# Attention with a memory beside a SiLU layer: products issued in halves, seven score-weight buffers, and a new order of the pieces

## The chip, the cores and the metric

The kernel runs on one core of a Trainium2 chip. The metric is the device time of one execution in microseconds (us). The page of the profile and its trace come from one execution of the kernel before, with every instruction's time. The engines are named as the profile names them: PE (TensorE, matrix products), PEld (its weight loads), DVE (VectorE), ACT (ScalarE), POOL (GpSimd) and SP (SyncE, which here issues nearly all DMAs).

## The reference, cut to what matters

The input x has 2048 rows of 512 numbers. After a layer norm, two branches read it; their sum and x are the output.

```
xn = layernorm(x)
# branch A: 32 heads of 16, four segments s of 512 rows
q, k, v = xn @ wq, xn @ wk, xn @ wv
for s in range(4):                       # M and z begin at 0
    a_dot = softmax(q_s k_s^T / 4 + causal mask) @ v_s
    a_mem = (phi(q_s) @ M) / (phi(q_s) @ z + 1e-6)
    o_s   = g * a_mem + (1 - g) * a_dot      # g = sigmoid(beta)
    M, z  = M + phi(k_s)^T @ v_s, z + sum(phi(k_s))
# branch B
h = silu(xn @ w1)                        # 512 -> 1792
out = x + o @ wo + h @ w2
```

phi(t) is t + 1 for t > 0 and exp(t) otherwise. All inputs are bf16.

## The kernel before, in words

**Tiles.** The 2048 rows are 16 tiles of 128; four tiles make a segment. xnT holds the normed input transposed, four blocks of 128 features on the partitions. The first four tiles are transposed by PE, the other twelve by DMA. "Head group" dt (0 to 3) is a block of 128 features of q, k or v, thus eight heads.

**Pieces.** All work is cut into pieces, each a small function. The string ORDER (lines 16 to 98) lists them by name, and a loop at the end (line 715) calls them one by one. Each engine executes its own instructions in exactly the order in which the pieces were called; semaphores between engines are added by the framework, which also gives out buffers. So ORDER, written out by hand, decides what stands behind what on every engine and in SP's queue. The names:

- `v`, `k`, `q`, `h` (s.i): a projection or first-layer unit of segment s: a 128x512 result in one PSUM bank, summed over four full products (128x128 weights, 512 columns; lines 301 and 332).
- `kv`/`ka`, `qv`/`qa`, `vv`/`va`: DVE or ACT copies that result out of the bank (lines 316, 326, 338). For k, POOL also makes a copy with the even heads' rows zeroed (kTo, line 317).
- `ha`: ACT takes tanh of a unit (line 419). `hv`: DVE makes silu of it into hT (line 424) and thereby frees the bank.
- `S` t: scores. Four 32-row groups of PE work side by side on 512 columns into psS, a single PSUM tile of four banks (line 597), and ACT takes the exponential of all of it into a weight buffer Pb (line 604, 128x2048, 80 of them). POOL sets the masked part to 0 (line 612). t = 20 s + 5 dt + b; the five batches b of a head group are the even and odd heads against the four key tiles.
- `E`, `O` n: weighing of even or odd heads of head group n = 4 s + dt: 16 small products of Pb and v into one bank (line 631). `Ev`/`Ea`, `Ov`/`Oa` copy it out and move the softmax sums by DMA (lines 646, 654, 661, 665).
- `fp`, `fa`, `fv` and `gp`, `ga`, `gv`: phi of k and of q on POOL, ACT and DVE. `t`: a DMA transposes phi(k). `m`: 8 products for M (line 381). `mv`, `mw`: DVE adds and masks M. `s`, `sv`: sums phi(q) z.
- `r`, `w` and, in the last segment, `R`, `W`: reciprocals and gate on DVE. `z`, `d`: DMAs that spread these factors over the partitions (line 504, two issues each). `zv`, `dv`: DVE multiplies with them. `n`, `nv`: one product with M and its addition on DVE (lines 530, 537).
- `o` s.j.i: one full product of the output of tile j in segment s: i = 0 to 13 is the unit hT[i] with w2, i = 14 to 17 the head group i - 14 with wo (line 572). 18 of them make an output tile. `xl`: loads x again. `st`: DVE adds x (line 550) and SP stores it (line 553).
- `xs`, `xg`, `Nv`, `X`, `XD`: layer norm statistics, root, normed tile, transposes by PE or DMA.

**Buffers.** Four PSUM banks (pool pp, tag "pb", function bank) serve all results of `v k q h E O m s n o` in turn; the other four are psS. In the last segment the output tiles j = 2 and 3 are gathered in two banks of psS, as the scores no longer need it (lines 560 to 565). Five buffers Pb (line 619) are given out by the order: `S` takes the first of a list, and the last weighing that reads a buffer puts it back.

**Around the change** the order is this: some 20 full products come ahead of the first score piece; then score pieces follow with other pieces between them, one small ACT job to nearly each; behind the last score piece (S79) come the rest of the units, the last two weighings and 78 output products, with the last segment's memory part.

Of the kernel before, what the change touches and what calls it, by code (L numbers as in the profile page):

```python
# [10 lines left out]
BF16 = mybir.dt.bfloat16  # L11
# [5 lines left out]
busy41 xs0 xg0.1 xs1 xg1.1 Nv0 X0.1 Xa0.1 busy10 xs2 xg2.1 xs3 xg3.1 v0.0 Nv1 X1.1 Xa1.1 Nv2 X2.1 Xa2.1 Nv3 X3.1 Xv3.1 v0.1 va0.0 odd k0.0 xs7 q0.0 qv0.0 q0.1 ka0.0 xs4 fa0.0  # L17
S1 xs5 q0.2 vv0.1 k0.2 kv0.2 qa0.1 fp0.2
S0 ones0 xs6 v0.3 fa0.2 xs8 xg4.4 vv0.3 qv0.2 h0.4
S3 xs11 k0.1 h0.7 ha0.7 kv0.1 xs9 hv0.7  # L20
S2 h0.10 Nv5 ha0.4 Nv4 XD4 v0.2 vv0.2
S4 h0.5 zeros fp0.1 ha0.10 Nv6 XD6 E0 xs10 hv0.4 XD5
S7 h0.2 Ev0 hv0.10 q0.3 ha0.5 xg8.4 fv0.2 fp0.0
S6 hv0.5 Nv7 XD7 O0 v1.1 Ov0 ha0.2 qv0.3
S5 xs14 h0.0 ha0.0 hv0.2 kind vv1.1 h0.1 fv0.0 Nv10
S9 k1.2 XD10 q1.3 kv1.2 ha0.1
S12 hv0.0 t0.0 k0.3 Nv11 E1 fa0.1 xs15 qv1.3 hv0.1 Ev1 kv0.3
S8 h0.11 Nv8 ha0.11 t0.2 ones1 tanh k1.1
# [12 lines left out]
S20 m0.0 sv0 xg12.4 ha1.4 o0.0.9 o0.0.12 r0.1 hv1.8 r0.3 k2.1 t0.3 mv0.0 r0.2
S24 kv2.1 o0.0.7 hv1.4 h1.0 E4 r0.0 ha1.0
S26 Ev4 o0.0.3 h1.1 O4 hv1.0 ha1.1 Nv15
S29 w0 z0.1 o0.0.13 gv1.1 z0.3 Ov4 k2.0 z0.2 h1.10 ha1.10 Nv12 kv2.0
S25 XD12 hv1.1 gp1.0 m0.2 h1.5 hv1.10 zv0.3 fp1.0 ha1.5 h1.13
S27 o0.0.8 mv0.2 v2.1 hv1.5 Nv13 z0.0 ha1.13 vv2.1 v2.0
S28 hv1.13 h1.6 E5 gv1.0 vv2.0 Ev5 ha1.6 hv1.6 o0.0.17 fp1.3
S32 v2.2 vv2.2 h1.2 o0.1.1 ha1.2 zv0.2
S34 o0.1.4 h1.3 XD15 hv1.2 o0.1.10 fa1.3 zv0.0 O5
S30 o0.1.2 zv0.1 xl0.0 o0.0.14 Ov5 fv1.3 o0.1.5 o0.1.11 o0.2.17 o0.0.15 fp1.2 o0.2.1 o0.1.3 o0.0.16 ha1.3  # L50
S31 o0.2.16 o0.1.14 fa1.2 o0.2.2 t1.1 XD13 Nv14 o0.2.15 hv1.3 o0.1.15 v2.3 st0.0
S33 vv2.3 q2.3 fa1.0 o0.2.11 o0.1.6 E6 fv1.2 qv2.3
S38 Ev6 h1.12 ha1.12 o0.1.16 o0.2.7 fp2.1 O6 Ov6
S36 o0.2.3 hv1.12 mw0.2 fa2.1 o0.2.9 o0.2.5 fv1.0 o0.2.12 xl0.3 q2.2 o0.1.13 xl0.2 qv2.2
S37 t1.3 o0.2.14 q2.0 ga1.2 o0.2.4 o0.3.7 qv2.0 o0.1.17 o0.2.8
S35 k2.3 o0.2.0 o0.3.0 o0.2.6 o0.2.10 fv2.1 gp1.3 ga1.3 t1.2 mw0.0 o0.3.13
S39 o0.1.7 gp1.2 o0.2.13 t1.0 o0.3.9 o0.1.12 o0.1.0 o0.3.8 kv2.3 gv1.3 E7
S41 Ev7 o0.3.17 o0.3.5 o0.1.9 XD14 o0.3.10 o0.1.8 st0.1 o0.3.15 o0.3.1 o0.3.4 ga2.3 o0.3.2
S40 O7 xl1.3 gv1.2 gp2.3 m1.2 o0.3.11 o0.3.14 fa2.2 st0.2 mv1.2 s1
S42 m1.0 Ov7 gv2.3 mv1.0 o0.3.16 o0.3.3 q3.1 qv3.1 o0.3.6 sv1 t2.1  # L60
S43 q3.3 fa2.0 qv3.3 o0.3.12 o1.1.12 fp2.0 st0.3 E8 r1.2
S44 v3.1 r1.0 q3.0 r1.3 va3.1 Ev8 o1.1.9
S46 r1.1 fv2.0 o1.1.3 w1 fp2.2 o1.1.6 z1.3 h2.8 qv3.0 O8 d1.3 ha2.8 hv2.8 t2.0
S47 h1.7 ha1.7 d1.2 o1.1.10 k3.0
S45 o1.1.8 Ov8 kv3.0 hv1.7 v3.2 k3.1 zv1.3 d1.1 ga2.2 vv3.2
S48 h2.3 z1.1 gp2.0 kv3.1 fv2.2 dv1.3 ha2.3 fp2.3 v3.0 o1.1.13
S49 vv3.0 n1.3 fa2.3 o1.1.5 hv2.3 nv1.3 v3.3 E9
S50 o1.1.17 h2.0 ha2.0 vv3.3 h2.2
S52 o1.1.0 o1.1.7 fv2.3 Ev9 xl1.2 k3.2 dv1.1 ha2.2 hv2.0 d1.0 zv1.1 mw1.2 kv3.2 hv2.2 z1.0 O9 z1.2
S54 Ov9 t2.2 o1.1.4 o1.0.0 o1.1.11 o1.1.2 q3.2 o1.0.13  # L70
S51 o1.0.7 qv3.2 n1.1 h2.4 o1.0.11 dv1.0 zv1.0 dv1.2 ha2.4 o1.0.17 gp2.2 o1.0.10
S53 o1.0.3 xl1.0 xl1.1 o1.0.9 nv1.1 o1.0.1 o1.0.6 hv2.4 n1.0 o1.0.2 nv1.0 E10 Ev10 zv1.2 ga2.0
S55 h2.11 o1.1.1 n1.2 ha2.11 nv1.2 o1.0.4 hv2.11 o1.1.15 gv2.2 mw1.0 o1.0.8
S56 O10 o1.1.16 h2.7 o1.0.5 Ov10 ha2.7
S58 hv2.7 o1.0.16 o1.1.14 gv2.0 o1.3.1 o1.3.10 o1.3.8 o1.3.11 o1.0.14 o1.3.17 o1.3.2 t2.3 ga2.1 gp2.1 st1.1 o1.3.13
S57 h2.1 m2.0 o1.3.7 o1.3.3 mv2.0 o1.0.15 ha2.1
S59 o1.0.12 h2.5 o1.3.6 hv2.1 st1.0 ha2.5 E11
S60 h2.6 o1.3.14 gv2.1 ha2.6 gp3.3 Ev11 hv2.5 O11 s2
S61 o1.3.0 xl2.2 Ov11 o1.3.12 hv2.6 o1.2.17 xl3.0 o1.2.8 sv2 r2.0 o1.3.9 h2.10 r2.2 gp3.1 ha2.10
S64 o1.2.16 o1.2.12 o1.3.5 o1.2.6 h2.12 ha2.12 hv2.10 o1.2.14 r2.3 o1.3.4  # L80
S62 h2.9 ha2.9 o1.2.9 o1.3.15 o1.2.4 o1.2.13 r2.1 o1.3.16 o1.2.2 o1.2.10 hv2.12 w2 d2.1
S63 d2.2 o1.2.3 hv2.9 o1.2.5 m2.2 st1.3 ga3.3 o1.2.1 z2.1 fill o2.2.12 d2.0 E12 mv2.2
S67 o2.2.1 o1.2.11 Ev12 h2.13 O12 gv3.3 dv2.1 ha2.13 Ov12 hv2.13
S66 o1.2.0 o2.2.7 o1.2.15 n2.1 dv2.0 o1.2.7 o2.2.3 o2.2.11 o2.2.13 o2.2.6 z2.2 o2.2.9
S65 st1.2 o2.2.4 o2.0.1 h3.4 o2.0.11 ha3.4 zv2.1 dv2.2 nv2.1 d2.3 z2.0 o2.0.6 o2.0.9 hv3.4 z2.3
S69 gp3.0 h3.3 ha3.3 o2.2.2 o2.2.5 E13 Ev13
S68 o2.2.10 o2.0.4 hv3.3 o2.2.0 h3.0 ha3.0 n2.2 o2.2.8 xl3.1 o2.0.8 zv2.2 nv2.2
S73 o2.0.10 k3.3 o2.2.16 hv3.0 ka3.3 h3.1 ha3.1 dv2.3 zv2.0
S70 hv3.1 O13 o2.0.0 zv2.3 o2.0.7 o2.0.3 n2.3 o2.0.13 o2.0.12 Ov13 o2.2.15 nv2.3 ga3.1
S71 n2.0 h3.2 nv2.0 o2.0.5 o2.1.11 o2.1.2 mw2.2 o2.2.17 xl2.0 gv3.1 o2.2.14 ha3.2 ga3.2 o2.0.16  # L90
S72 o2.1.8 o2.0.14 o2.0.15 st2.2 h3.5 mw2.0 ha3.5 gp3.2 o2.1.0 o2.0.2 o2.1.10
S74 hv3.2 ga3.0 o2.1.12 hv3.5 o2.1.5 o2.0.17 o2.3.3 o2.1.7 o2.3.7 gv3.2 st2.0 E14
S76 o2.3.5 gv3.0 o2.1.16 o2.1.3 xl2.3 o2.3.12 o2.3.0 Ev14 O14 s3 xl2.1 Oa14
S75 o2.3.2 o2.1.1 sv3 h3.9 o2.3.10 h3.10 r3.0 ha3.9 ha3.10
S77 o2.1.15 r3.2 r3.1 r3.3 o2.1.14 o2.3.1 w3 hv3.9 hv3.10 o2.3.4 h3.11 ha3.11 o2.3.13 o2.3.8
S78 o2.3.9 o2.3.11 d3.3 R0.1 o2.1.9 d3.1 hv3.11 R0.2 h3.12 R0.0 R0.3 o2.3.15 o2.3.16 ha3.12 o2.1.17
S79 E15 W0 d3.0 hv3.12 o2.1.6 o2.1.4 z3.2 o2.3.6 h3.7 Ea15 o2.1.13 o2.3.14 st2.1 h3.13 ha3.7 hv3.7 dv3.3 ha3.13 o3.3.0 o3.3.1 hv3.13 O15 dv3.0 o2.3.17 h3.8 ha3.8 z3.0 d3.2 dv3.1 o3.2.4 o3.0.3 o3.0.2 Ov15 o3.0.11 h3.6 o3.3.3 hv3.8 ha3.6 o3.3.4 zv3.2 st2.3 o3.1.0 xl3.2 o3.1.10 hv3.6 o3.1.9 o3.1.13 o3.2.7 R1.2 n3.1 o3.1.11 o3.0.4 o3.1.6 R1.1 o3.2.8 o3.1.3 dv3.2 o3.3.13 o3.0.7 o3.2.13 o3.3.11 o3.2.10 n3.2 z3.1 o3.0.0 o3.0.8 R1.0 o3.3.8 o3.2.11 zv3.0 o3.0.5 nv3.2 o3.1.8 R1.3 W1 o3.1.4 o3.3.12 n3.0 o3.0.9 o3.0.6 o3.3.9 nv3.0 o3.3.5 o3.2.9 o3.1.5 o3.1.14 z3.3 o3.2.16 o3.0.10 o3.2.12 o3.0.16 o3.3.2 zv3.1 nv3.1 n3.3 zv3.3 o3.2.0 nv3.3 xl3.3 o3.0.15 o3.3.6 o3.0.13 o3.1.16 o3.0.1 o3.1.15 o3.0.17 o3.2.6 o3.0.12 o3.0.14 o3.3.7 st3.0 o3.3.16 o3.3.17 o3.3.14 o3.1.12 o3.3.10 o3.3.15 o3.2.14 o3.2.3 o3.2.5 o3.1.17 o3.1.7 o3.1.2 o3.2.15 o3.1.1 st3.3 st3.1 o3.2.1 o3.2.2 o3.2.17 st3.2
# [4 lines left out]
def kernel(  # L102
# [196 lines left out]
    def mm4(ps, w_sb, cols, rhs):  # L299
        for ki in range(DT):  # L300
            nc.tensor.matmul(  # L301
                ps[:, :], lhsT=w_sb[:, ki, cols], rhs=rhs(ki), start=(ki == 0), stop=(ki == DT - 1)
            )

    def dense(s, w_sb, i):

        ps = bank([P, L], F32, "ps")
        mm4(ps, w_sb, slice(i * P, (i + 1) * P), lambda ki: xnT[:, ki, s * L : (s + 1) * L])
        return ps

    def k_mm(s, dt):
        sts[s]["k", dt] = dense(s, wk_sb, dt)
# [9 lines left out]
    def q_mm(s, dt):  # L322
        sts[s]["q", dt] = dense(s, wq_sb, dt)
# [4 lines left out]
    def v_mm(s, j):  # L328
        t = s * TPS + j
        ps = sts[s]["v", j] = bank([P, L], F32, "ps")  # L330
        for ki in range(DT):
            nc.tensor.matmul(  # L332
                ps[:, :], lhsT=xnT[:, ki, t * P : (t + 1) * P], rhs=wv_sb[:, ki, :],
                start=(ki == 0), stop=(ki == DT - 1),
            )
# [76 lines left out]
    def h_mm(s, ft):  # L412
        if "hT" not in sts[s]:
            sts[s]["hT"] = hpool.tile([P, FT, L], BF16, name="hT", tag="hT")
        sts[s]["h", ft] = dense(s, w1_sb, ft)
# [333 lines left out]
```

## Time and profile before

| | us |
|---|---|
| median of three runs (lowest, highest) | 235.81 (235.72, 236.08) |
| the profiled execution | 235.23 |
| its span, from the first instruction to the last | 233.4 |
| PE busy, of the span | 219.8 |
| ACT busy; of it the 80 exponentials at 1.877 | 196.4; 150.1 |
| DVE busy | 171.5 |
| POOL busy | 117.4 |
| first exponential begins, last begins | 13.40, 206.73 |
| last product begins | 229.71 |

Busy time of PE joins overlapping products: one 128x512 product shows 0.38 us from its start to its end, but in a run of them the next starts 0.2157 us later. In the timeline a row has the start, the length, the engine, the line of the kernel, and in brackets the idle time ahead of it with what ended that. In a table of stretches the columns are PE, PEld, DVE, ACT and POOL busy (with the number of instructions), granted clock of PE, share and rate of the DMAs. A row of waits has the sum, the number and the longest.

### The profile page before, as it was taken

Reading aid. Unit: us, or ns where it says so; the run is one execution under the profiler, and the core shown is the slowest. Engines: PE = TensorE matmul, PEld = TensorE weight load, DVE = VectorE, ACT = ScalarE, POOL = GpSimd, SP = SyncE. Lnnn points to the kernel's source line nnn. Section 1 sums busy time; section 2 is a strip of 40 time slices with the busy share of each in tenths; the row PEclk is TensorE's granted clock in tenths of the full one; section 3 lists DMA queues with packets and bytes.
Section 4 is the critical chain, followed back from the end, with each engine's and each line's share of the span. In section 5 each row is a group of like instructions: output and inputs, shape, how many; then the busy total and the mean of one; then the engine's idle time right before and its main releaser. Section 6 shows DMA issues by size and latency. Waiting matters only on the chain.

```text
span 233.4 us, 4991 instructions
## 1 busy us (share of the span) xinstructions
PE 219.8 (94%) x1845; PEld 94.2 (40%) x1879; DVE 171.5 (73%) x343; ACT 196.4 (84%) x172; POOL 117.4 (50%) x181
## 2 busy tenths in 40 slices
PE   7998798999999999999999999999999999999993
PEld 7533333433343443333434333344443334344440
DVE  3588999765689887767697887855775695868843
ACT  2478899999999999999999998999998999983000
POOL 4348767674448763546757766345624535440000
PEclk9999999999999999999999999999999999999998
DMA  6999532113101122204432121321130312132211
GB/s 203 369 376 344 128 32 51 26 36 68 37 9 31 49 67 60 58 31 97 113 59 68 47 80 55 75 53 53 52 98 26 101 36 87 41 93 69 90 56 69
DMA packets 34632, 20.38 MB, mean 87 GB/s; under 512 B 15664, under 2 KB 34096, under 8 KB 34608
## 3 DMA queue, kind: packets, MB, share of 16 engines
q1 hardware_dynamic: 34320, 19.80, 30.2%
q8 instruction: 14, 0.23, 0.4%
q10 hardware_dynamic: 288, 0.26, 0.4%
q14 instruction: 10, 0.08, 0.1%
HBM read 9.96 MB, written 2.10 MB: 52 GB/s over the span
## 4 chain that ended last, share of the span: by engine, by line
PE 70%; ACT 12%; DMA 6%; issue 4%; DVE 4%; SPq 2%
PE ps L301 23%; PE psO L572 22%; ACT Pb L604 9%; PE psS L597 9%; PE psV L631 6%; DMA x_hi<-in_A_x_dram 6%; PE ps L332 4%; PE psS L572 3%; ACT th L419 3%; PE psM L381 1%; PE ps L530 1%; DVE stats L269 1%; SPq L176 1%; ACT ex L355 1%; DVE xn_t L283 1%
## 5 line engine op out<-in xcount | busy, mean ns | idle before, releaser
L604 ACT ACTIVATE Pb<-psS 128x2048 bf16<-128x2048 f32 x80 | 150.1, 1877 | 6.4 <-PE psS L597 5.6
L612 POOL TENSOR_SCALAR_AFFINE_SELECT Pb<-Pb 128x512 bf16<-128x512 bf16 (+1 forms) x112 | 81.0, 736 | 81.9 <-ACT Pb L604 80.6
L301 PE MATMUL ps<-xnT,w_sb 128*128 128x512 bf16 x217 | 56.3, 380 | 1.9 <-DVE hT L424 0.7
L572 PE MATMUL psO<-w_sb,hT 128*128 128x512 bf16 x182 | 56.2, 381 | 0.9 <-issue 0.6
L424 DVE SCALAR_TENSOR_TENSOR hT<-th,ps 128x512 bf16<-128x512 bf16 x56 | 37.8, 678 | 13.8 <-ACT th L419 13.4
L419 ACT ACTIVATE th<-ps 128x512 bf16<-128x512 f32 x56 | 33.2, 594 | 4.5 <-PE ps L301 4.4
L572 PEld LDWEIGHTS <-hT 128*128 128x128 bf16 x224 | 20.3, 97 | 27.1 <-issue 7.9
L301 PEld LDWEIGHTS <-w_sb 128*128 128x128 bf16 x224 | 20.4, 98 | 26.1 <-issue 5.5
L631 PE MATMUL psV<-Pb,Vz 128*32 128x384 bf16 (+3 forms) x512 | 23.3, 302 | 0.6 <-DVE Vz L338 0.6
L597 PE MATMUL psS<-qT,kT 16*128 16x384 bf16 (+3 forms) x256 | 17.3, 302 | 2.0 <-ACT Pb L604 0.9
L597 PE MATMUL psS<-qT,kTo 32*128 32x512 bf16 (+3 forms) x256 | 17.2, 300 | 1.7 <-ACT Pb L604 1.0
L572 PE MATMUL psO<-wo_sb,oT 128*128 128x512 bf16 x51 | 17.6, 381 | 0.3 <-issue 0.3
L631 PEld LDWEIGHTS <-Vz 128*32 128x32 bf16 x512 | 10.8, 96 | 17.4 <-issue 7.3
L301 PE MATMUL ps<-xnT,wk_sb 128*128 128x512 bf16 x62 | 16.2, 380 | 0.3 <-DVE oT L537 0.2
L332 PE MATMUL ps<-wv_sb,xnT 128*128 128x512 bf16 x61 | 16.2, 381 | 0.3
L301 PE MATMUL ps<-xnT,wq_sb 128*128 128x512 bf16 x62 | 16.1, 381 | 0.1
L317 POOL TENSOR_SCALAR kTo<-kT,pm_odd 128x512 bf16<-128x512 bf16 x16 | 12.1, 757 | 5.1 <-ACT kT L316 3.4
L661 DVE CAST odd<-psV 128x512 bf16<-128x512 f32 x15 | 10.3, 685 | 4.6 <-PE psV L631 4.6
L654 DVE CAST oraw<-psV 128x512 bf16<-128x512 f32 x15 | 10.3, 684 | 4.0 <-PE psV L631 3.8
L326 DVE CAST qT<-ps 128x512 bf16<-128x512 f32 x15 | 10.2, 683 | 4.0 <-PE ps L301 4.0
L597 PEld LDWEIGHTS <-kT 16*128 16x128 bf16 x256 | 6.1, 91 | 17.0 <-issue 15.7
L550 DVE SCALAR_TENSOR_TENSOR o_out<-psO,x_res 128x512 bf16<-128x512 f32 x14 | 9.6, 685 | 4.3 <-PE psO L572 4.1
(83 smaller groups left out, 225.5 us busy)
## 6 DMA issues: line engine op xcount, KB each, us to landing
w_sb<-in_B_w_dram SPq DMA_DIRECT2D x2, 1792.0 KB
spr<-rz SPq DMA_DIRECT2D x56, 64.0 KB
x_res<-in_A_x_dram SPq DMA_DIRECT2D x16, 128.0 KB
out_dram<-o_out SPq DMA_DIRECT2D x16, 128.0 KB
x_hi<-in_A_x_dram SPq DMA_DIRECT2D x2, 512.0 KB
oraw<-odd SPq DMA_DIRECT2D x64, 16.0 KB
wv_sb<-in_A_wv_dram SPq DMA_DIRECT2D x2, 256.0 KB
wk_sb<-in_A_wk_dram SPq DMA_DIRECT2D x1, 512.0 KB
```

Source lines behind the costliest of these rows:

```text
L301: nc.tensor.matmul(ps[:, :], lhsT=w_sb[:, ki, cols], rhs=rhs(ki), start=(ki == 0), stop=(ki == DT - 1))
L317: nc.gpsimd.tensor_scalar(out=kTo[:, dt, :], in0=kT[:, dt, :], scalar1=pm_odd[:, 0:1], scalar2=1.0, op0=ALU.mult, op1=ALU.mult,)
L332: nc.tensor.matmul(ps[:, :], lhsT=xnT[:, ki, t * P : (t + 1) * P], rhs=wv_sb[:, ki, :], start=(ki == 0), stop=(ki == DT - 1),)
L419: nc.scalar.activation(out=th[:], in_=sts[s]["h", ft][:, :], func=AF.Tanh, scale=0.5)
L424: nc.vector.scalar_tensor_tensor(out=st["hT"][:, ft, :], in0=st.pop(("th", ft))[:], scalar=1.0, in1=st.pop(("h", ft))[:, :], op0=ALU.add, ...
L572: nc.tensor.matmul(st["psO", j], lhsT=lhsT, rhs=rhs, start=len(done) == 1, stop=len(done) == FT + DT)
L597: nc.tensor.matmul(psS[:, g, c0 : c0 + nq], lhsT=kk[rows, dt, kt * P : (kt + 1) * P], rhs=st["qT"][rows, dt, kt * P : L], start=True, stop ...
L604: exp = nc.scalar.activation(out=Pb[:, :, :], in_=psS[:, :, :], func=AF.Exp, scale=SCALE)
L612: mask = nc.gpsimd.affine_select(out=blocks, in_=blocks, compare_op=ALU.is_ge, fill=0.0, base=0, pattern=[[0, blocks.shape[1]], [1, P]], c ...
L631: nc.tensor.matmul(psV[32 * g : 32 * g + 32, kt * P : L], lhsT=Vzs[s % 2][:, kt, 4 * dt + g, par : par + 2, :].rearrange("p a d -> p (a d) ...
L654: copy(out=oraw[:], in_=sts[s].pop(("psV", 0))[:, :])
L661: copy(out=odd[:], in_=sts[s].pop(("psV", 1))[:, :])
```

## The change

1. The pieces `v k q h` are cut in two: `k0.1.0` issues the first two products of a unit, `k0.1.1` the other two; the bank is taken by the first half.
2. There are seven weight buffers Pb instead of five.
3. The products of output tile 2 of the last segment no longer wait for DVE's reading of tile 3, and the other way round: the framework sees the two banks as one tile, and a declaration takes the dependence away.
4. ORDER is written anew. It has the same pieces (those of point 1 in halves), with few exceptions: which engine copies some results (`qa0.0` and `ka0.2` in place of `qv0.0` and `kv0.2`, `qv0.1` in place of `qa0.1`, `ka3.1` and `ka3.2` in place of `kv3.1` and `kv3.2`, `kv3.3` in place of `ka3.3`, `Ov14` and `Oa15` in place of `Oa14` and `Ov15`), and where each piece stands. Behind the last score piece (now S78) stand 87 full products instead of 98.

The functions:

```diff
-    def mm4(ps, w_sb, cols, rhs):
-        for ki in range(DT):
+    def half_mm(s, key, part, lhsT, rhs):
+
+        if part == 0:
+            sts[s][key] = bank([P, L], F32, "ps")
+        for ki in (2 * part, 2 * part + 1):
             nc.tensor.matmul(
-                ps[:, :], lhsT=w_sb[:, ki, cols], rhs=rhs(ki), start=(ki == 0), stop=(ki == DT - 1)
+                sts[s][key][:, :], lhsT=lhsT(ki), rhs=rhs(ki), start=(ki == 0), stop=(ki == DT - 1)
             )
...
-    def k_mm(s, dt):
-        sts[s]["k", dt] = dense(s, wk_sb, dt)
+    def k_mm(s, dt, part):
+        dense(s, "k", wk_sb, dt, part)
...
-        nc.vector.scalar_tensor_tensor(
+        st["out", j] = nc.vector.scalar_tensor_tensor(
...
-        nc.tensor.matmul(st["psO", j], lhsT=lhsT, rhs=rhs, start=len(done) == 1, stop=len(done) == FT + DT)
+        mm = nc.tensor.matmul(st["psO", j], lhsT=lhsT, rhs=rhs, start=len(done) == 1, stop=len(done) == FT + DT)
+        if s == LAST and j >= 2 and ("out", 5 - j) in st:
+            tc.declare_no_dep(mm.ins, st["out", 5 - j].ins, reason="the two outputs lie in banks of their own")
...
-    Pbs = [ppool.tile([P, 4, L], BF16, name=f"Pb{i}") for i in range(5)]
+    Pbs = [ppool.tile([P, 4, L], BF16, name=f"Pb{i}") for i in range(7)]
```

The order, its beginning and its end (the first line's opening, up to `va0.0`, keeps its order but for the halves):

```diff
-... v0.1 va0.0 odd k0.0 xs7 q0.0 qv0.0 q0.1 ka0.0 xs4 fa0.0
-S1 xs5 q0.2 vv0.1 k0.2 kv0.2 qa0.1 fp0.2
-S0 ones0 xs6 v0.3 fa0.2 xs8 xg4.4 vv0.3 qv0.2 h0.4
-S3 xs11 k0.1 h0.7 ha0.7 kv0.1 xs9 hv0.7
-S2 h0.10 Nv5 ha0.4 Nv4 XD4 v0.2 vv0.2
-S4 h0.5 zeros fp0.1 ha0.10 Nv6 XD6 E0 xs10 hv0.4 XD5
+... v0.1.0 v0.1.1 va0.0 odd k0.0.0 k0.0.1 ka0.0 q0.0.0 q0.0.1 xs7 k0.1.0 vv0.1 kind ones0 qa0.0 fa0.0
+S3 k0.1.1 v0.3.0 k0.2.0 k0.2.1 xs5 xs6 ka0.2 xs4 xg4.4 fp0.0
+S4 q0.1.0 kv0.1 v0.3.1 h0.4.0 h0.4.1 ha0.4 vv0.3 hv0.4 zeros Nv5 Nv4
+S0 Nv7 h0.10.0 h0.10.1 Nv6 q0.1.1 v0.2.0 ha0.10 fp0.1
+S2 qv0.1 fv0.0 hv0.10 h0.5.0 XD5 h0.5.1 XD6 v0.2.1 q0.2.0 ha0.5
+S5 vv0.2 q0.2.1 h0.7.0 h0.7.1 xs11 ha0.7 v1.1.0 hv0.5 xs9
+S1 h0.1.0 v1.1.1 qv0.2 xs10 fp0.2 hv0.7 k0.3.0 XD7 h0.1.1 XD4 t0.0 ha0.1
...
+S78 z3.0 dv3.2 h3.6.0 o2.1.1 o2.1.0 zv3.2 h3.6.1 ha3.6 h3.10.0 h3.10.1 d3.1 st2.1 o3.2.7 hv3.6 o3.3.8 o3.3.2 E15 Ea15 zv3.0 O15 o3.1.2 o3.1.11 ha3.10 ... o3.3.17 o3.3.1 st3.3 ... o3.1.17 st3.0 st3.2 st3.1
```

## The prediction

> **What bounds the kernel now.** I read the page first, then the stretches, then the timeline. The page says that TensorE is busy 94% of the span and that its clock is granted in full until the last slice; ACT has 84%.
>
> ```profile
> PE 219.8 (94%) x1845; PEld 94.2 (40%) x1879; DVE 171.5 (73%) x343; ACT 196.4 (84%) x172; POOL 117.4 (50%) x181
> ...
> PEclk9999999999999999999999999999999999999998
> ```
>
> The table of stretches of 5 us shows that this share is a mean over stages: DVE is full at 25 us (4.96 of 5), ACT at 45 us (4.99, while PE has 4.50), and near 145 us PE and ACT together.
>
> ```profile
> 25.00:30.00 5.00, 4.17 (x57) 1.86 (x58) 4.96 (x11) 4.28 (x5) 4.35 (x9) 1.00 0.43 88
> 45.00:50.00 5.00, 4.50 (x46) 1.85 (x45) 2.76 (x6) 4.99 (x5) 3.16 (x5) 1.00 0.09 21
> 145.00:150.00 5.00, 4.95 (x58) 2.10 (x58) 3.71 (x7) 4.99 (x5) 1.67 (x3) 1.00 0.38 91
> ```
>
> The timeline tells why ACT is full. There is one score buffer (psS). PE may write the next scores when the exponential has read the last ones, and meanwhile ACT does one small job (0.59 us):
>
> ```profile
> 45.99 1.88 ACT L604 ACTIVATE Pb<-psS 128x2048 bf16<-128x2048 f32 x1
> ...
> 47.76 0.59 ACT L419 ACTIVATE th<-ps 128x512 bf16<-128x512 f32 x1
> ...
> 47.91 0.40 PE L597 MATMUL psS<-qT,kTo 32*128 32x384 bf16 x8 [0.36 <-ACT Pb L604]
> ...
> 48.36 1.88 ACT L604 ACTIVATE Pb<-psS 128x2048 bf16<-128x2048 f32 x1
> ```
>
> So exponentials start every 2.37 to 2.38 us (45.99, 48.36, 50.73), whatever PE has to do, as long as its work fits between two score pieces. PE here waited 0.36. **The 80 exponentials cut the run into 79 intervals, each as long as the longer of 2.377 and PE's own work in it.**
>
> PE's prices come from intervals above that floor. Intervals with 9, 10 and 11 full products (128x512) take 2.38, 2.59 and 2.81, so a product costs 0.2157 and a score piece 0.44. The interval 40.79 to 43.61 holds a score piece, 8 products and one weighing (E or O): 2.82, so a weighing costs 0.656. Two neighbours (2.53 and 2.46), one of them with 8 products and a memory product (m), give 0.45 for that one; a sums piece (s) is about 0.2. Summed over the words of ORDER:
>
> | intervals | products, before / after | weighings | PE work | paced sum, before / after | measured before |
> |---|---|---|---|---|---|
> | 1-12 | 84 / 94 | 4 / 3 | 26.0 / 27.5 | 29.0 / 29.0 | 30.2 |
> | 13-26 | 96 / 99 | 6 / 6 | 31.3 / 32.4 | 33.3 / 33.4 | 33.3 |
> | 27-56 | 229 / 226 | 11 / 12 | 71.4 / 70.9 | 71.8 / 71.5 | 71.8 |
> | 57-79 | 189 / 192 | 9 / 9 | 58.1 / 58.7 | 58.1 / 59.1 | 58.1 |
> | after the last | 98 / 87 | 2 / 2 | 22.5 / 20.1 | | 23.2 |
>
> From interval 13 on the prices give the measured time to 0.1. Only the first stage is 1.2 above, and the waits name its cause: products that wait for a bank which DVE has not yet emptied. The fourth line is at the very end.
>
> ```profile
> PE ps L301 <- DVE hT L424: 0.7, 1, 0.7
> PE psV L631 <- DVE Vz L338: 0.6, 1, 0.6
> PE ps L301 <- DVE Vz L338: 0.5, 1, 0.5
> PE psS L572 <- DVE o_out L550: 0.6, 1, 0.6
> ```
>
> **The change part by part.** The instructions stay the same: 716 full products, 80 score pieces, 32 weighings. Only the slack can change.
>
> *Pieces of two products and the new order.* Before, 26 intervals offer 2.377 but hold only 57.3 us of PE work for 62.3. A piece of four fits or does not; there are not yet output products to fill with. After, the same 26 intervals hold 193 products where 180 were, in the same paced time (62.4): 13 more products (+2.80), one more memory product (+0.45), one weighing fewer (-0.66). What is done here is missing at the end: 87 products after the last exponential instead of 98, **-2.37 us** (11 x 0.2157). Against it the paced sum of all 79 intervals rises from 192.1 to 193.0, **+0.9**. The cut itself I cost at nothing: near 220 us the products alternate between two banks one by one (psO at 221.21 and 221.42, psS at 221.64, psO at 221.85) at the same pitch of 0.21 to 0.22. If the cover for that were wrong, 0.01 on each of 104 cut pieces would be 1 us.
>
> *Changes of form.* A score piece has 512 columns, which a full product streams in 0.2157, and costs 0.44: some 0.11 for each of its two changes between full products and small ones. Counted in ORDER the changes fall from 198 to 191, worth 0 (the prices hold it, as weighings stand beside scores in both) to -0.8. I take 0, as the prices fit, and -0.4 for the low end. The Trainium skill, "TensorEngine Tiling (Array Packing)", Key Properties, says that a change of the tiling mode drains TensorE; by that rule alone the sum would be 0.8 us lower, and the 0.44 agrees with it.
>
> *First exponential.* k0.0's products end at 10.96, ACT's copy at 11.57, POOL's odd copy at 12.37. Before, the query copy was queued behind DVE's statistics, which waited 1.66 for x; the scores started at 12.95, the exponential at 13.40. Now ACT copies the queries at 11.85 to 12.43 and the first scores need the odd copy (12.37), so the exponential starts near 13.0: **-0.4**.
>
> *Excess of the first stage.* I went through DVE's queue by hand with its pitches (statistics 0.81, copies 0.60, phi 0.84, norm 0.5). Up to the twelfth interval its work falls from 27.5 to 26.1. No bank comes over 0.1 us late; one interval has two small ACT jobs and PE work of 2.60, which costs 0.2, and another waits 0.2 for h0.1's tanh. Excess 0.6 instead of 1.2: **-0.6**. Bounds: 0 (all hidden) to 1.4 (one copy late by 0.6 more, at 0.65 each).
>
> *Seven score-weight buffers.* No exponential of before waits for a buffer (the listed waits of ACT at L604 are all for the scores), so two more take away no wait; they only allow the order. Cost 0.
>
> *Last two outputs independent.* The tail shows the wait:
>
> ```profile
> 228.53 0.69 DVE L550 SCALAR_TENSOR_TENSOR o_out<-psS,x_res 128x512 bf16<-128x512 f32 x1 [2.33 <-PE psS L572]
> ...
> 229.28 0.59 PE L572 MATMUL psS<-w_sb,hT 128*128 128x512 bf16 x2 [0.57 <-DVE o_out L550]
> ...
> 230.12 0.69 DVE L550 SCALAR_TENSOR_TENSOR o_out<-psS,x_res 128x512 bf16<-128x512 f32 x1 [0.30 <-PE psS L572]
> ```
>
> The wait goes: **-0.57**. Late next is DVE: the last two outputs become ready 0.65 apart and take 0.69 each: **+0.08**. The fourth output reuses the buffer of the first, which is stored some 2 us ahead; the last store's data are through 1.3 us after its issue (230.84 to 232.1), so that holds.
>
> *The tail's chain.* The last quarter's sums go through SP's queue, then reciprocal, spread, product, addition, then o3.3.17. Before, it took 12.8 us from O15's last product (211.35) to the last addition (224.17), behind five other issues of SP (210.35 to 213.56). After, O15 ends 4.6 us behind the last score piece and o3.3.17 is due at 17.5. By SP's queue in the new order (spreads of z3.0 and d3.1, a store, then the sums at 6.1 to 7.2) the addition ends at 15.8: 1.7 us to spare; with the old length, 0.1. I take no wait. Three places (the banks of E15, of O15 and of n3.2) have only 0.1 to 0.2 to spare; for these I add **+0.4**.
>
> Sum: -2.37 + 0.9 - 0.4 - 0.6 - 0.57 + 0.08 + 0.4 = **-2.6**. The profiled execution took 235.23 (span 233.4, 1.8 around it) and would take 232.6. The runs shown have a median of 235.81, 0.6 above it; I forecast **233.2** for the median.
>
> **The rivals.** *Banks held open (slower).* Four banks serve all products. In the new order 43 pieces begin before a score piece and end behind it, seven of them in the first seven intervals, and none did before: such a bank is held 2.4 us longer. If the next product then finds no bank until one more DVE copy is through, at 0.65 as in the waits above, seven cost 4.5 us: 237.7. It decides against the change from four such waits (2.6 / 0.65). For it: DVE has 4.9 of 5 between 20 and 40 us. Against: DVE's load there falls, and by hand each bank was free. Chance 0.14.
>
> *The tail's chain takes over.* With SP's issues 1.5 us worse than my count and the old length, PE waits some 1.4 before o3.3.17: 234.6. Against it speak the 1.7 to spare. Chance 0.12.
>
> *The halves fill nothing.* If the 13 products moved forward only push the scores back, the -2.37, the +0.9 and the +0.4 go, -0.6 too: 234.9 remains, from the first exponential and the last outputs. Against: the paced sum of 26 intervals does not grow. Chance 0.08.
>
> *The clock.* The only slice below full is the last, 0.8 over 5.8 us, worth 1.2 us. If finer bank changes made PE pause so that three such slices came up, 3.6 us would be lost: 236.8. The row speaks against it: at 220 us the bank changes with each product and the clock is 1.00. Chance 0.02. The Trainium skill, "TensorE: Matmul & The Clock Gate", section "A second HAM failure mode: psum-queue depth-cycling", warns of just this; before's trace does not show it.
>
> **How the numbers follow.** My case has 0.62, with its own range 231.8 (no excess and no small waits, -1.0; changes of form, -0.4) to 234.4 (excess 1.4, small waits 0.8). Nothing changed has 0.02. The range reaches from 231.8 to 235.3, which takes in the two rivals that only shrink the gain. A difference under 0.2% (0.5 us) can hardly be told from none here. Faster 0.81, same 0.04, slower 0.15.
>
> **What would show it.** Right: first exponential near 13.0; intervals of 2.38 up to the 60th; the 27th exponential near 76.0 (before 76.87); the last near 206.6, as before (206.73), but with some 20 us of products behind it instead of 23; no wait of L571 for L549. Wrong: waits of L304 for DVE in the first 45 us (banks), a wait of L571 for the addition L536 near the end (chain), a clock below 9 inside the page's row. The forecast fails if the early waits exceed 3 us in sum.

## The result and the profile after

| | before | after |
|---|---|---|
| median, beside each other in one session (us) | 235.76 (235.17 to 236.08, 4 executions) | 238.61 (237.97 to 239.46, 4 executions) |
| the profiled execution; its span | 235.23; 233.4 | 237.97; 236.3 |
| first, 27th, last exponential begins | 13.40, 76.87, 206.73 | 13.28, 79.91, 211.79 |
| last product begins; last addition (DVE) begins | 229.71; 230.12 | 231.55; 231.98 |

The ratio is 1.0126 with an interval of 1.0088 to 1.0164: **1.3% slower**, where 233.2 (1.1% faster) was forecast, and above the top of the range, 235.3. The sign is wrong. Of three kernels below (the loads moved, only wo moved, only the exchange) one execution each took over 1.5% more than the fastest and is left out of the ratio, so a ratio need not be the quotient of the medians.

The page of after shows about the same work in a longer span (rows as before: busy time, share, instructions; then granted clock of PE in 40 slices):

```profile
PE 219.3 (93%) x1846; PEld 93.3 (39%) x1879; DVE 176.4 (75%) x341; ACT 197.6 (84%) x174; POOL 119.1 (50%) x181
...
PEclk9999999999999999999999999999999999999998
```

The three stretches that the prediction showed, now of after, tell where to look. The first has 2.72 of PE's 5 us and 2.03 of ACT's; the second has PE at 4.93, where it had 4.50, as the forecast wanted; the third is full as before.

```profile
25.00:30.00 5.00, 2.72 (x17) 1.02 (x19) 3.32 (x8) 2.03 (x3) 0.36 (x1) 1.00 0.81 117
45.00:50.00 5.00, 4.93 (x30) 1.72 (x31) 4.28 (x9) 3.84 (x4) 2.64 (x5) 1.00 0.32 64
145.00:150.00 5.00, 4.96 (x47) 2.01 (x45) 4.04 (x7) 4.87 (x5) 3.06 (x5) 1.00 0.23 49
```

The list of PE's waits (sum, number, longest) names what stands in the hole: not a bank, but a transposed tile of the input that a DMA had not yet brought.

```profile
PE ps L304 <- DMA xnT<-xn_t: 3.0, 1, 3.0
...
PE ps L304 <- DVE qT L330: 0.9, 1, 0.9
...
PE psM L380 <- DMA phiK<-pk: 0.5, 1, 0.5
```

The timeline of after shows the transposes' issue and the product that waited:

```profile
13.10 6.53 SPq L176 DMA_DIRECT2D wo_sb<-in_A_wo_dram  x1
...
19.75 7.09 SPq L682 DMA_TRANSPOSE xnT<-xn_t  x4
...
27.13 0.61 PE L304 MATMUL ps<-wv_sb,xnT 128*128 128x512 bf16 x2 [3.00 <-DMA xnT<-xn_t]
```

The first of the four transposes is tile 5's (XD5). It is issued at 19.75; the product v1.1.0 that reads the tile starts at 27.13. SP's row before it is the issue of the load of wo, and w2 (1792 KB) stands ahead of that. In before the first transposes were issued at 24.32.

**Interval by interval.** The prices of the prediction (0.2157 for a product, 0.44 for a score piece, and so on, at least 2.377) give a paced sum of 193.0 for after. It took 198.5 (211.79 - 13.28): a lag of 5.5. It does not lie spread out: 2.96 in the fifth interval (tile 5), 0.92 in the twelfth (the wait for qT), 0.47 in the 41st (phiK), 0.50 in the 70th, 0.39 in the 30th; 68 of the 79 agree with their price to 0.1. I call this difference from the paced sum the lag below. Before had 1.2.

### The profile page after: what moved, and what is told of

Its sections match the earlier page's. It is cut to its first block, busy times and chain, and to the rows that moved or that the text cites. A ratio compares the mean times of both kernels' runs of the same rounds, so it can differ in the third digit from the quotient of the medians.

```text
span 236.3 us, 4980 instructions
## 1 busy us (share of the span) xinstructions
PE 219.3 (93%) x1846; PEld 93.3 (39%) x1879; DVE 176.4 (75%) x341; ACT 197.6 (84%) x174; POOL 119.1 (50%) x181
## 3 DMA queue, kind: packets, MB, share of 16 engines
q1 hardware_dynamic: 34320, 19.80, 31.1%
## 4 chain that ended last, share of the span: by engine, by line
PE 57%; ACT 16%; DVE 9%; DMA 8%; issue 5%; POOL 1%; SPq 1%; DVEq 0%
PE ps L304 22%; PE psO L571 17%; ACT Pb L605 12%; PE psS L598 7%; PE psV L632 5%; DMA xnT<-xn_t 4%; PE psS L571 3%; DMA spr<-rz 3%; ACT th L418 2%; DVE xn_t L283 2%; ACT ex L354 2%; DVE hT L423 2%; DMA x_lo<-in_A_x_dram 1%; PE ps L529 1%; PE psM L380 1%
## 5 line engine op out<-in xcount | busy, mean ns | idle before, releaser
L613 POOL TENSOR_SCALAR_AFFINE_SELECT Pb<-Pb 128x512 bf16<-128x512 bf16 (+1 forms) x112 | 80.0, 728 | 85.1 <-ACT Pb L605 85.0
L304 PE MATMUL ps<-xnT,w_sb 128*128 128x512 bf16 x218 | 59.4, 380 | 0.4 <-DVE oraw L655 0.2
L571 PE MATMUL psO<-w_sb,hT 128*128 128x512 bf16 x183 | 57.7, 380 | 1.1 <-issue 0.8
L571 PEld LDWEIGHTS <-hT 128*128 128x128 bf16 x224 | 20.8, 98 | 27.2 <-issue 6.6
L304 PE MATMUL ps<-wv_sb,xnT 128*128 128x512 bf16 x59 | 17.4, 380 | 3.6 <-DMA xnT<-xn_t 3.0
L571 PE MATMUL psO<-wo_sb,oT 128*128 128x512 bf16 x54 | 18.7, 380 | 0.4 <-issue 0.3
L598 PE MATMUL psS<-qT,kT 16*128 16x256 bf16 (+3 forms) x256 | 17.3, 301 | 1.6
L304 PE MATMUL ps<-xnT,wq_sb 128*128 128x512 bf16 x60 | 17.5, 381 | 1.3 <-DVE qT L330 0.9
L598 PE MATMUL psS<-qT,kTo 32*128 32x256 bf16 (+3 forms) x256 | 17.2, 299 | 0.7 <-ACT qT L330 0.2
L321 POOL TENSOR_SCALAR kTo<-kT,pm_odd 128x512 bf16<-128x512 bf16 x16 | 13.4, 840 | 4.3 <-ACT kT L320 3.4
L337 DVE CAST Vz<-ps 128x512 bf16<-128x512 f32 x14 | 9.6, 683 | 3.2 <-PE ps L304 3.1
```

Source lines behind the costliest of these rows:

```text
L304: nc.tensor.matmul(sts[s][key][:, :], lhsT=lhsT(ki), rhs=rhs(ki), start=(ki == 0), stop=(ki == DT - 1))
L321: nc.gpsimd.tensor_scalar(out=kTo[:, dt, :], in0=kT[:, dt, :], scalar1=pm_odd[:, 0:1], scalar2=1.0, op0=ALU.mult, op1=ALU.mult,)
L571: mm = nc.tensor.matmul(st["psO", j], lhsT=lhsT, rhs=rhs, start=len(done) == 1, stop=len(done) == FT + DT)
L598: nc.tensor.matmul(psS[:, g, c0 : c0 + nq], lhsT=kk[rows, dt, kt * P : (kt + 1) * P], rhs=st["qT"][rows, dt, kt * P : L], start=True, stop ...
L613: mask = nc.gpsimd.affine_select(out=blocks, in_=blocks, compare_op=ALU.is_ge, fill=0.0, base=0, pattern=[[0, blocks.shape[1]], [1, P]], c ...
```

## The experiments

Theory T: the new order is as good as forecast, but a few things that the new order wants earlier come late: above all DMA transposes that stand behind other transfers. Rival B is the prediction's own: banks held open by half-finished pieces. Rival Q: SP's queue as a whole is the limit, and a wait cured in one place comes back in another. For each group there is its edit, the expectation on record, and the measurement. Ratios are to before, run beside it.

### Loads moved behind the early transposes

In after, the loads of w2 and wo are taken from the kernel's head and issued as a piece of their own behind tiles 5, 6, 7, 4 and the first phi(k):

```diff
-    load_w(nc.sync, w2_sb, B_w2, 0, FT)
-    load_w(nc.sync, wo_sb, A_wo, 0, DT)
...
-S1 h0.1.0 v1.1.1 qv0.2 xs10 fp0.2 hv0.7 k0.3.0 XD7 h0.1.1 XD4 t0.0 ha0.1
+S1 h0.1.0 v1.1.1 qv0.2 xs10 fp0.2 hv0.7 k0.3.0 XD7 h0.1.1 XD4 t0.0 lw ha0.1
```

> The changed kernel, with the loads of w2 and wo (2.3 MB) issued by SP behind the transposes of tiles 5, 6, 7 and 4 instead of ahead of them. Theory (the transposes' data stand in the DMA queue behind those loads): the loads run at about 0.35 MB/us and the queue was empty of them at 24.2, so without the two it is empty near 17.5; the transpose of tile 5, issued near 19.7, lands near 22.4, and the 3.0 us wait of the product v1.1 (L304 for xnT) is gone: 235.6, from 234.8 to 236.2. Rival 1 (banks held open by halves): the wait only shows up at the next place, 238 to 239. Rival 2 (four transposes take over 4 us by themselves, whatever stands ahead): some 1 to 1.5 us of the wait stay, 236.6 to 237.2.

Measured: 237.20 (10 executions) beside 236.24; ratio 1.0044 (1.0015 to 1.0073). The wait for tile 5 is gone. The table of stretches shows what moved at the time (the last columns are granted clock, DMA share and GB/s). After:

```profile
22.00:24.00 2.00, 1.86 (x11) 0.69 (x10) 1.97 (x6) 1.99 (x3) 1.92 (x3) 1.00 1.10 349
24.00:26.00 2.00, 0.13 (x1) 0.00 (x0) 1.97 (x6) 1.14 (x2) 0.96 (x2) 1.00 1.92 174
26.00:28.00 2.00, 0.87 (x11) 0.24 (x11) 1.43 (x4) 0.00 (x0) 0.00 (x0) 1.00 1.00 199
```

With the loads moved, and below it the start of v1.1.0 there:

```profile
22.00:24.00 2.00, 1.86 (x12) 0.72 (x11) 2.00 (x5) 1.99 (x3) 1.92 (x3) 1.00 0.45 90
24.00:26.00 2.00, 1.80 (x15) 0.72 (x14) 1.93 (x5) 1.99 (x3) 0.90 (x2) 1.00 0.53 107
26.00:28.00 2.00, 1.63 (x14) 0.50 (x12) 1.97 (x5) 1.51 (x2) 0.57 (x1) 1.00 0.57 82
...
24.30 0.59 PE L302 MATMUL ps<-wv_sb,xnT 128*128 128x512 bf16 x2
```

In after the loads run at 349 GB/s until 24 us and PE then stands still (0.13 of 2). Without them the transposes are issued at the same time (19.80), and v1.1.0 starts at 24.30 without a wait. So it was the loads ahead in the DMA queue, not SP's issue and not DVE's norm. This is shown. The Trainium skill, "DMA: Bandwidth & Descriptors", section "Queues, rings and completion order", says that each DMA engine consumes its descriptors in ring order; these rows agree.

The rate of all 16 DMA engines in after, in 40 slices of 0.35 us from 16 to 30 us (GB/s), shows why tile 5 came as late as 27.13:

```profile
GB/s 351 345 354 339 372 299 325 348 351 351 345 354 348 351 345 354 345 339 348 351 354 345 350 334 304 204 68 23 22 86 285 250 252 253 34 200 142 1 0 0
```

From 25.45 to 26.15 there are 22 to 23 GB/s, a sixteenth of 349: it looks as if one engine alone was still at its share of the loads. The packets in the trace agree. Those of the loads have 1024 bytes, those of the transposes 256, 512 to a tile. In order of time, 502 of the first 512 have started by 25.30 and the last ten start from 26.07, when the last packet of the loads has ended; with the loads moved all 512 start between 21.10 and 21.86.

But the time fell by 1.9 (by the ratios, 0.0082 of 236), not by 3. The 237.20 lies just where rival 2 had it (236.6 to 237.2), but no wait for the tile is left; instead, a new wait stands in the 41st interval. The timeline:

```profile
112.39 1.27 SPq L370 DMA_TRANSPOSE phiK<-pk  x1
...
112.56 0.39 PE L378 MATMUL psM<-Vz,phiK 128*128 128x128 bf16 x4
...
114.93 0.40 PE L378 MATMUL psM<-Vz,phiK 128*128 128x128 bf16 x4 [1.98 <-DMA phiK<-pk]
```

m1.2 needs the transpose t1.3, which SP issues at 112.39; the product that reads it starts 2.5 us later. In the trace its 512 packets start between 1.25 and 2.02 us behind the issue, and so they do in after, so nothing shows that it waits behind other transfers' data; it is issued late. In after it was issued at 113.01, and PE, which came there later by its 3.0 us, waited only 0.49. The early wait had hidden the late one.

Only wo moved, w2 left at the head:

```diff
-    load_w(nc.sync, wo_sb, A_wo, 0, DT)
...
+        "lw": lambda: load_w(nc.sync, wo_sb, A_wo, 0, DT),
```

> The changed kernel, with only the load of wo (0.5 MB) issued behind those four transposes, w2 ahead as it was. Theory of the queue: 0.5 MB at 0.35 MB/us is 1.5 us, so the wait of v1.1 falls from 3.0 to about 1.5 and the time to about 237.1. Rivals 1 and 2: no change, 238 to 239.

Measured: 239.68 (4 executions), ratio 1.0118 (1.0046 to 1.0189); a miss. The wait for tile 5 fell to 1.2, near the expected size, but this is luck: the last packet of the loads ended at 25.45 and v1.1.0 started at 26.55, only 0.6 sooner than in after, and PE came to it 1.3 later, mostly by a wait of 0.86 for DVE's copy of k. The wait for phiK rose to 2.4, and a stretch of lower clock behind it cost 1.1 more (below).

The same move in before, where both loads go behind its last early transpose:

```diff
-S6 hv0.5 Nv7 XD7 O0 v1.1 Ov0 ha0.2 qv0.3
+S6 hv0.5 Nv7 XD7 lw O0 v1.1 Ov0 ha0.2 qv0.3
```

> The kernel before, with the loads of w2 and wo behind its transposes of tiles 4 to 7. Theory of the queue: its transposes are issued at 24.3, when the loads are through, and its v1.1 waits only 0.4 for them; so at most 0.4 is gained, 235.3 to 235.8. If the loads cost more than this wait, for instance through SP's queue or DMA sharing, it gains 1 or more.

Measured: 235.82, ratio 0.9995 (0.9969 to 1.0021): nothing. Before issues its transposes at 24.3 (here 24.5), when the loads are nearly through: their last packet ends at 25.9, and the transposes' first starts 1.3 behind the issue in both. So the price belongs to the new order and not to the loads alone.

### The norm beside POOL's memset

The kernel with the loads moved; in ORDER, `ones1` goes from the interval of S14 to that of S12:

```diff
-S14 ones1 h0.11.1 k1.2.0 ha0.11 k1.2.1 fp0.3 kv1.3 hv0.2 tanh kv1.2 E1
+S14 h0.11.1 k1.2.0 ha0.11 k1.2.1 fp0.3 kv1.3 hv0.2 tanh kv1.2 E1
...
-S12 Ov1 v1.0.1 fv0.3 vv1.0 k1.0.0 h0.6.1 XD9 ha0.6 k1.0.1
+S12 ones1 Ov1 v1.0.1 fv0.3 vv1.0 k1.0.0 h0.6.1 XD9 ha0.6 k1.0.1
```

> As the changed kernel with the late loads, and besides the memset of the ones columns of the second value tile on POOL (0.95 us) is moved from the interval behind S14 to that behind S12. In the changed kernel the normed tile 11 on DVE took 1.54 us instead of 0.40, all of it while POOL was busy with that memset and a mask, and a product then waited 0.94 for a bank which DVE had not emptied. Theory (POOL's memset holds DVE's norm): the wait of 0.94 goes, 0.9 us below the kernel with late loads alone, 234.7. Rival (the wait is set by DVE's amount of work, 3.4 us in an interval of 2.6, whatever POOL does): no difference to the kernel with late loads.

Measured: 236.42 (10 executions), ratio 1.0008 (0.9974 to 1.0042): 0.8 below the kernel with the loads moved, with overlapping intervals, and above the 234.7 expected. The timeline of after shows the cause of the 0.92: a norm of a tile on DVE, the query copy queued behind it, and PE, which needs that copy's bank.

```profile
40.32 1.54 DVE L283 TENSOR_SCALAR xn_t<-x_hi,mv_all,rstd_all 128x512 bf16<-128x512 bf16 x1
...
40.77 0.95 POOL L712 MEMSET Vz<- 128x1024 bf16 x1
...
44.92 1.02 PE L304 MATMUL ps<-xnT,wq_sb 128*128 128x512 bf16 x4 [0.94 <-DVE qT L330]
```

With the loads moved alone the norm is as long (first row), and the wait is 0.93. With `ones1` moved too the norm is short (second row), and the wait for the bank is gone:

```profile
38.15 1.54 DVE L281 TENSOR_SCALAR xn_t<-x_hi,mv_all,rstd_all 128x512 bf16<-128x512 bf16 x1
...
37.49 0.65 DVE L281 TENSOR_SCALAR xn_t<-x_hi,mv_all,rstd_all 128x512 bf16<-128x512 bf16 x1
```

The lag of the twelfth interval fell from 0.91 to 0, but that of the 41st and 42nd rose to 3.2, 0.66 of it at a lower clock (below): again PE came sooner to the same late transpose.

### The late transpose itself

t1.3 (due in S40) and t1.0 (due in S41) exchange places, so that SP issues t1.3 ahead of the six transfers of Ov6:

```diff
-S34 E6 t1.0 v2.3.0 xl0.2 k2.3.1 t1.1 Ev6 gv1.0 gp1.1 h1.12.0
+S34 E6 t1.3 v2.3.0 xl0.2 k2.3.1 t1.1 Ev6 gv1.0 gp1.1 h1.12.0
...
-S37 Ov6 hv1.12 o0.2.8 t1.3 o0.2.3 q2.0.0 h1.2.0 gv1.1 q2.0.1 qv2.0 fa2.2 o0.3.15
+S37 Ov6 hv1.12 o0.2.8 t1.0 o0.2.3 q2.0.0 h1.2.0 gv1.1 q2.0.1 qv2.0 fa2.2 o0.3.15
```

In after alone:

> The changed kernel with one change of order: the transposes of phi(k) for the second segment's head group 3 (t1.3, due first) and head group 0 (t1.0, due later) exchange places, so that the first of them no longer stands in SP's queue behind the six transfers of Ov6. Theory of two late transposes: the wait of m1.2 for phiK (0.49) goes, the wait for tile 5 (3.0) stays; some 0.5 less than the changed kernel, 238.1, last exponential near 211.3. Rival (SP's queue as a whole is the limit, so that the wait only passes to m1.0): no change, 238.6. Rival (a late wait absorbs whatever is saved early): the same as the first, so this run tells only the first two apart.

Measured: 238.69 beside 236.10, ratio 1.0096 (1.0061 to 1.0132). Its interval overlaps after's, so the 0.5 cannot be told from the times; in the profile the wait for phiK is gone and the wait for tile 5 (2.9) stays.

With the loads moved as well, thus the kernel of the first experiment with the same exchange:

> The changed kernel with the loads of w2 and wo issued behind the early transposes, and t1.3 and t1.0 exchanged. Theory of two late transposes: without the exchange the saving of 3.0 at tile 5 was taken back by the wait for phiK (2.0 in the profiled execution, and in some executions a lower clock behind it). With both cured, the lag against the prices falls from 4.7 to some 2.5, the last exponential comes near 208.8, and the time is 234.9 (ratio to before 0.995). Rival (SP's queue as a whole): the wait passes to m1.0 or to later transfers, 236.5 to 237. Rival (banks held open are the main loss): 237.

Measured: 235.08 (12 executions), ratio 0.9945 (0.9919 to 0.9970). The lag is 2.5, the last exponential begins at 208.62. Moving the loads is now worth 3.6 us (ratio 1.0096 to 0.9945, of 236) where it was worth 1.9 with the late transpose in place; by the intervals, each is uncertain by about 1.

With `ones1` moved too, as shown above, so that all three edits are in:

> The run before with the memset of ones for the second v buffer moved from the interval of S14 to that of S12, so that the norm of tile 11 on DVE no longer runs beside it. Theory: the wait of 0.94 for the query copy goes as well; lag 1.0 to 1.5, last exponential near 207.5, granted clock 0.996 or more in nearly all runs, and the time 233.6 to 234.0 (ratio 0.990 to 0.993): the forecast's time, from the forecast's own sum, once the two transposes and one copy are not late. Rival (SP's queue as a whole): a wait elsewhere of 1 to 2.5, 235 to 236.4.

Measured: 234.21 (11 executions), ratio 0.9907 (0.9878 to 0.9936), which overlaps the run before. The twelfth interval's 0.9 is gone; in the profiled execution the lag is still 2.5, over the expected 1.0 to 1.5, as 0.65 and 0.31 came up in the 42nd and 44th intervals. **The kernel with all its halves and its order, but three things in other places, is 0.9% faster than before.** Rival Q holds for a small part: of the waits for phiK, 0.8 came back at m1.0, which reads the exchanged t1.0. PE's longest waits behind the first exponential:

```profile
PE psM L378 <- DMA phiK<-pk: 0.8, 1, 0.8
PE ps L302 <- DVE kT L318: 0.6, 1, 0.6
```

Last, kv2.0 set ahead of the norm of tile 13:

```diff
-S28 fv1.1 hv1.5 o0.0.0 k2.0.0 k2.0.1 Nv13 o0.1.2 ga1.1 o0.1.12 h1.1.0
-S29 kv2.0 E5 zv0.3 zv0.0 ...
+S28 fv1.1 hv1.5 o0.0.0 k2.0.0 k2.0.1 kv2.0 Nv13 o0.1.2 ga1.1 o0.1.12 h1.1.0
+S29 E5 zv0.3 zv0.0 ...
```

> The run before with kv2.0 ahead of the norm of tile 13 on DVE instead of behind it. The wait of the weighing E5 for that copy (0.4) goes: 0.3 to 0.4 less than the run before if nothing waits for tile 13 in turn; if the transposes of tile 13 are then late, no gain. Only the mean of ten runs could show so little.

Measured: 233.90 (6 executions), ratio 0.9899 (0.9871 to 0.9927). The wait of E5 for that copy is gone and the lag is 1.8; the difference from the run before is inside the intervals. This is the fastest version, and it beats both kernels.

### The halves

The kernel with the loads moved, each unit whole again at the place of its second half, over the whole of ORDER:

```diff
-S4 q0.1.0 kv0.1 v0.3.1 h0.4.0 h0.4.1 ...
-S0 Nv7 h0.10.0 h0.10.1 Nv6 q0.1.1 v0.2.0 ...
+S4 kv0.1 v0.3.0 v0.3.1 h0.4.0 h0.4.1 ...
+S0 Nv7 h0.10.0 h0.10.1 Nv6 q0.1.0 q0.1.1 ...
```

> As the changed kernel with late loads, but each first half is moved to where its second half stands, so that no piece is cut. By the prices of the prediction (score piece 0.44, product 0.2157, weighing 0.656, floor 2.377) the paced sum of the 79 intervals rises from 193.0 to 201.6, as intervals then hold 7 or 11 products instead of 9. Theory (only the sum of products per interval counts): 8 to 9 us above the kernel with late loads, some 244. Rival (PE makes up within neighbours, as a short interval follows a long one): under 4 us.

Measured: 242.48, ratio 1.0269 (1.0247 to 1.0291). The paced sum by the prices is 201.6 instead of 193.0, and the profile has 203.0 from first to last exponential (13.53 to 216.50): a lag of 1.4. The 8.6 of the prices came as computed; the time rose only by 5.3, between the two forecasts (8 to 9, and under 4), because the lag fell by 3.3, as PE now comes later to the same transposes. So in this order the halves do fill the gaps, and the prices hold for an order that I had not priced them on. That no order of whole units does as well is not shown: before's, written for them, has a paced sum of 192.1, though with 11 more products behind it.

### The other parts

The declaration taken out of after:

```diff
-        if s == LAST and j >= 2 and ("out", 5 - j) in st:
-            tc.declare_no_dep(mm.ins, st["out", 5 - j].ins, reason="the two outputs lie in banks of their own")
```

> The changed kernel without the declaration that the last two outputs are independent. Theory: the products of tile 2 behind the first store wait for DVE's 0.69 us, so PE waits 0.6 to 0.9 near the end and the time is 0.6 to 0.9 above the changed kernel: 239.3. Rival (DVE or the stores set the end): no difference.

Measured: 239.97 (4 executions), ratio 1.0178 (1.0125 to 1.0231). The wait of L571 for L549 is back (0.6) in the profile; the intervals of the two kernels overlap, so the times do not show it. The rest of the difference between the profiled executions is lag (6.2 against 5.5), with 1.5 of the 6.2 in a stretch of lower clock behind tile 5's wait. The same two lines alone put into before, with the two names that they use:

> The kernel before with that declaration alone. Theory: its wait of 0.57 on PE near the end goes, 0.5 to 0.6 below before: 235.2. Rival: DVE's three last additions queue up and give back half of it.

Measured: 235.11 (10 executions) beside 235.98, ratio 0.9965 (0.9944 to 0.9986): the 0.57 of the prediction, within the interval, and in the profile the wait is gone. Seven buffers alone in before (`range(5)` becomes `range(7)` for Pbs):

> The kernel before with seven score-weight buffers and nothing else. Theory: no exponential of before waits for a buffer, so no difference, within 0.5 us, and the exponentials start at the same times. Rival (a hidden wait for a buffer): first stage shorter by over 0.3.

Measured: 235.68, once, beside 235.98: no difference that could be told; the first and last exponentials begin at 13.31 and 206.92.

## Why the prediction was wrong, point by point

In the profiled executions the span was to fall by 2.6 and rose by 2.9, a miss of 5.5. Its parts: 0.3 first exponential, 2.96 tile 5, 0.92 tile 11's norm, 1.0 other early and middle waits, -0.7 tail up to the last addition, 1.0 end.

- **Failed: the excess of the first stage** ("No bank comes over 0.1 us late ... Excess 0.6"). I followed DVE's queue by hand, but the step also moved XD5, XD6, XD7 and XD4 from 24.32 to 19.75, and I did not follow them into the DMA queue, where w2 and wo were still under way, at full rate until 24 us and with their last packets until 26. I silently took the old distance: in before the last packet of a tile starts 2.06 behind the issue, for tile 5 in after 6.45. So the wait for a transposed tile stood in the sum at nothing, and it was 2.96. I also gave every norm the same 0.5, although a norm took 1.54 beside POOL: 0.92. Before's own trace could have warned of it: two norms from 22.79 took 1.50 together, beside a mask of POOL of 1.10 at 23.05. The lag was to be 0.6 and was 5.5. The two loads moved, the exchange and `ones1` bring it to 2.5 and the time to 0.9907 of before, which is the forecast's 233.2 / 235.8 = 0.989 within the interval. That the time agrees is partly luck: in the profiled execution the lag is 1.9 over the forecast and the end 0.6 longer, the part behind the last exponential 0.7 shorter, and the span, 232.8, is only 0.6 below before's where the sum had 2.6.
- **Mis-sized: the small waits** (0.4 for three places in the tail). They came in the middle instead, at phiK, kv2.0 and tile norms, some 1.6 with the rest of the early ones. The one at phiK was the dangerous one: small in after (0.49), 1.9 to 2.4 as soon as PE is ahead of SP.
- **Mis-sized: the first exponential.** 13.28 instead of 13.0: k0.0's products began at 10.27, 0.34 later than in before, and the scores, which started at 12.84, waited last for ACT's copy of the queries (12.20 to 12.79) and not for the odd copy (12.03 to 12.73).
- **Right: 11 products fewer at the end, and the outputs independent.** From the last exponential to the last addition after took 20.19 and before 23.39: -3.20, where -2.37 - 0.57 + 0.08 was -2.86; no run shows where the other 0.3 comes from. PE no longer waits for L549:

```profile
231.31 0.69 DVE L549 SCALAR_TENSOR_TENSOR o_out<-psS,x_res 128x512 bf16<-128x512 f32 x1 [0.17 <-PE psS L571]
...
231.55 0.38 PE L571 MATMUL psO<-wo_sb,oT 128*128 128x512 bf16 x1
...
231.98 0.69 DVE L549 SCALAR_TENSOR_TENSOR o_out<-psO,x_res 128x512 bf16<-128x512 f32 x1
```

- **Left out: the end.** From the last addition to the span's end: 3.28 before, 4.32 after, 3.9 in the run with all three cures. After stores its last four outputs closer together (additions from 229.37 to 231.98, in before from 225.51 to 230.12). That the stores' transfers cause the 0.6 to 1.0 was not tried.
- **Right: the prices and the paced sum** (193.0; 201.6 with whole units), and nothing for seven buffers.
- **Rival, banks held open.** Its 237.7 came near, but for another reason. One long wait of that kind stood in the stage (0.94), and it came from a norm made slow. With every bank still held open, the cured kernel is faster than before. (The 43 of the prediction counts crossings: 39 pieces, four of them across two score pieces.)
- **Rival, the halves fill nothing:** no, as the run with whole units shows.
- **Rival, the tail's chain:** no such wait. **Rival, the clock:** not by bank changes. But two of after's four executions have a mean clock of 0.989 and 0.991, near the 0.988 to 0.990 of the profiled executions that have one stretch at half clock behind a wait, so part of the loss of the median may be clock (below).

What stays open: the rest of the lag in the cured version (1.8 to 2.5, against 0.6), the longer end, and why t1.3's transfer takes 1.25 us from the issue to its first packet and 0.5 from its last packet to the product.

## What to carry to other kernels

When an order moves a step forward, follow its transfers too: ask which bytes are still in the queue at the new time of issue, and not only when the issuing engine is free. A change can gain what it should and still lose, because one late transfer takes it all; compare interval by interval with a price model, and the loss shows as one line and not as a general slowness. And cure late transfers together: the one behind hides behind the one ahead, so that each cure alone is worth less than its part of both (here 1.9 for the loads and 0.7 for the exchange, the latter within the noise, and 4.3 together, by the ratios).

## What the runs showed of the hardware

**A wait of 2 to 3 us can cost twice.** In the kernel with the loads and `ones1` moved, PE waited 1.88 for phiK until 113.25. The stretches (clock is the third column from the end):

```profile
110.00:112.00 2.00, 1.38 (x22) 0.65 (x17) 1.93 (x3) 1.99 (x2) 0.26 (x2) 1.00 0.10 25
112.00:114.00 2.00, 0.61 (x4) 0.45 (x5) 0.10 (x1) 0.41 (x1) 0.59 (x1) 0.81 0.52 132
114.00:116.00 2.00, 1.78 (x28) 0.85 (x32) 0.39 (x2) 1.11 (x1) 0.00 (x0) 0.50 0.27 67
116.00:118.00 2.00, 1.88 (x30) 0.91 (x20) 1.54 (x3) 0.83 (x2) 1.11 (x2) 0.84 0.00 1
```

The clock is halved from about 113.2 to 116.6, 3.4 us (0.19, 0.5 and 0.16 of 2 us are missing, 1.7 in all, twice that at half speed), just when PE has work again. Stretches of the same 3.4 follow the wait of 2.4 in the run with only wo moved, that of 1.9 in the run without the declaration, and that of 2.9 in the run with only the exchange; no such stretch follows the 3.0 of after's profiled execution or the 1.98 with the loads moved. The trace's record of the clock suggests why: in the four runs the drop comes 105.81, 112.64, 20.48 and 20.48 us behind the moment at which the clock first became full, 31, 33, 6 and 6 times 3.413. On such a grid each of the four waits falls into one window (the 2.9 but for 0.07), while an edge divides the 3.0 of after into 1.9 and 1.1 and the 1.98 into 1.0 and 1.0. Of the ten executions of the kernel with the loads and `ones1` moved, six had a mean clock of 0.988 to 0.993 and took 236.4 to 237.8, four had 0.996 to 1.0 and took 235.0 to 235.9. After's four executions had 0.989 to 0.996; those of the three versions in whose profiled execution PE never waits 1 us behind the first exponential had 0.996 or more, all 29 of them. The Trainium skill, "TensorE: Matmul & The Clock Gate", section "Part 1: The HAM clock gate", speaks of a free-running window of about 3.4 us and of half clock after an idle one. The length and the grid agree. But no window was idle throughout here: 1.88 us of waiting in one was enough, and the 1.9 of after was not, so the length of the wait alone does not decide.

**A norm on DVE that starts beside POOL's memset or mask ends with it.** The shortest of after's twelve takes 0.40. The one that took 1.54 ended at 41.86, POOL's memset at 41.72; the one of 0.65 ended at 38.14, POOL's mask at 37.99. Not every instruction of POOL does this: in before a norm beside a phi of POOL (82.08, 0.61) took 0.44. The Trainium skill, "SBUF — State Buffer", section "SBUF: two separate sides", says that DVE, in some of its modes, and POOL lock a port pair they share, and the loser stands still; the first two rows agree.
